# One engine order for another in a gated mix of sliding-window attention and a token-mixing MLP

## The chip, the core and the metric

The kernel runs on one core of a Trainium2 chip. Its time is the device time of one execution in microseconds (us), and the figure that is compared is the median of several executions.

## What is computed

For 2048 tokens of 512 features, an attention `a` (32 heads of 16 features, causal window of 256 tokens) and an MLP `b` that mixes tokens are added with a gate per token:

```python
g = sigmoid((x * gate_w).sum(-1, keepdims=True))          # x: 1 x 2048 x 512
qkv = x @ wqkv                                            # wqkv: 512 x 1536, 32 heads of 16
scores = q @ k.T * 16 ** -0.5, kept where 0 <= i - j < 256
a = (softmax(scores) @ v) @ wo
h = layernorm(x)
u = gelu(einsum("bsd,sf->bdf", h, w1) + b1)               # f = 1376
b = transpose(einsum("bdf,fs->bds", u, w2) + b2)
out = g * a + (1 - g) * b
```

All inputs and the output are bf16.

## The kernel before

The work is cut into some 1100 small tasks, and the order in which each engine takes its tasks is written out by hand as lists of names, one for each engine (`PLAN`): PE is TensorE, ACT is ScalarE, DVE is VectorE, POOL is GpSimd, and SP is the queue that issues all loads and stores. A name may carry the numbers of the buffers that the task takes. `arrange` walks through these lists with a price for each task and emits the instructions engine by engine in that order; the prices decide only how the lists interleave in the program, not what stands in a list. `BLOCK`, `AHEAD`, `FETCH` and `BUSY` are its prices for fetching PE's instructions in blocks of 256; `LATENCY` is its price from an engine's end to the next engine's start.

The tasks, by name (j is one of 17 query stretches of 128 tokens, shifted by 64, the first and the last being halves; t a tile of 128 tokens; i a quarter of 512 tokens):

- `warm`, `warmb`: products of a zeroed tile (`zeros`, a memset on DVE), before the data are there. `xta0.*` transposes the first 512 tokens on PE, `xtc0.*` copies the result to `XT0`; the other quarters are loaded transposed by DMA (`xt1` to `xt3`).
- `x*`, `wqk*`, `wv`, `gw`, `w1_gi`, `w2_g`, `wo`, `bias`: loads. `wqk` holds the weights of q and k in four pieces, `wv` those of v, `gw` the gate's weights copied to all partitions.
- `q`, `k`, `v`, `u`, `y`: chains of full matrix products (`chain`, line 670), cut into steps of two products, each chain in one PSUM bank: `k3_0.2` is the step from product 2 of the third k group of quarter 0. `qc`, `kc`, `vc`, `ub`, `f` evict the bank on ACT or DVE. A step can run with the array tiled in four column groups, which takes four times the instructions; the set `THEN` says after which tasks this is done.
- `s{j}.v*`, `s{j}.C`, `s15.A`, `s15.B`: scores into a pair of PSUM banks, on 32 rows of the array; `e*` takes the exponential on ACT, `m*` the mask (on DVE as a product with a mask tile, or on POOL as an affine select), `pv{j}.*` the product with V. Then `n1` to `n4` and `nz` on DVE transpose, divide by the row sums and transpose back into `xo`.
- `bs`, `ba`, `pow`, `h`: the layer norm. All sixteen `h` are needed before the first `u` chain.
- `y{t}` sums the MLP's second product (11 weight chunks, the last of 96 rows) and the attention's output projection (4 chunks) in one chain of 15 products; `f{t}` applies the gate and bias in one eviction, `o{t}` stores. For the last tile, the chain is cut by columns: `y15l` and `y15r`, 256 columns each.
- The gate's logits: for quarter 0 on PE (`gate0`, 16 products of one column with the transposed `XT0`, line 802, then `gatem0`), for the other quarters on DVE (`gl4` to `gl15`, line 822, a product with `gw` summed over the row). `NGP` is the number of quarters that PE does. `gatee` is the exponential, `ez` spreads it for the attention's division, `gates` forms the two columns for `f`.

PE changes between four modes: full products (d), column-tiled products and `pv` (p), scores (s), corner scores (c); a half `pv` step is a fifth (h).

Of the kernel before, what the change touches and what calls it, by code (L numbers as in the profile page):

```python
# [9 lines left out]
ACT = mybir.ActivationFunctionType  # L10
# [68 lines left out]
SWITCH = 0.095  # L79

BLOCK, AHEAD, FETCH, BUSY = 256, 80, 3.6, 3.0
LATENCY = {"PE": 0.22, "ACT": 0.15, "DVE": 0.12, "POOL": 0.15, "SP": 2.0}


def arrange(tasks):
# [18 lines left out]
    mode, then = "d", "d"  # L104
    count, come, loads = AHEAD, {}, 0.0
    order = []
    while len(order) < len(tasks):
# [19 lines left out]
        t.cost = t.engines[e]  # L127
        ins = t.ins
        if e == "PE":
            new = then if t.flex else t.mode  # L130
            if new != mode:
                t.cost += SWITCH
            if t.flex and new == "p":
                t.tiled = True
                ins *= 4
            if t.mode != "d":
                then = "p" if t.name in THEN else "d"
            mode = new
        if e == "SP" and t.lat is not None and t.engines[e] > 1.0:
            loads = max(loads, start + t.cost + t.lat)  # L140
        if ins:
            block = count // BLOCK
            while (block + 1) * BLOCK <= count + ins:
                block += 1
                at = start + t.cost * (block * BLOCK - count) / ins
                wait = max(0.0, come.get(block, 0.0) - at)
                t.cost += wait
                come[block + 1] = at + wait + FETCH + (BUSY if at + wait < loads else 0.0)
            count += ins
# [41 lines left out]
        warm:3 xta0.0.0:7 xta0.0.1:6 warmb xta0.1.1:4 xta0.1.0:5 q1_0.0:2 k3_0.0:3 k1_0.0:6 q3_0.0:1 k0_0.0:7  # L191
        q3_0.1 q0_0.0:0 k3_0.1 q1_0.1 q1_0.2 k1_0.1 k3_0.2 k0_0.1 q0_0.1 q2_0.0:5 q1_0.3 q0_0.2 q1_0.4 q0_0.3
        k3_0.3 q3_0.2 q0_0.4 k3_0.4 q3_0.3 k2_0.0:4 q2_0.1 k0_0.2 k1_0.2 k1_0.3 k0_0.3 k1_0.4 q2_0.2 q3_0.4 q2_0.3
        k0_0.4 k2_0.1 k2_0.2 k2_0.3 k2_0.4 q2_0.4 s0.v0:62 q3_1.0:0 q3_1.2 k3_1.0:1 k3_1.2 q0_1.0:7 s0.C:42 v1.0:6
        q0_1.2 s-1.C:02 v1.2 v2.0:5 v2.2 s1.v3:02 biast:4 v0.0:7 v0.2 v3.0:5 v3.2 q1_1.0:4 s1.v0:62 v5.0:1 q1_1.2
        gate0:5 v5.2 v14.0:0 s0.v1:62 v13.0:5 k2_1.0:1 v14.2 pv-1.0:6 v10.0:4 k2_1.2 v13.2 s1.v2:26 k2_2.0:0 v10.2
        v15.0:1 v12.0:5 v12.2 v15.2 k2_2.2 pv0.0:2 pv0.1 s1.v1:64 pv0.2 v4.0:1 v4.2 k3_2.0:0 k3_2.2 s2.v1:26 v7.0:5
        v7.2 k0_2.0:4 s1.C:60 k0_2.2 v6.0:3 v6.2 s2.v3:06 k0_1.0:2 k0_1.2 k1_1.0:5 k1_1.2 pv1.0:6 pv1.1 pv1.2
        s2.v0:02 v11.0:4 v11.2 v8.0:5 v8.2 pv1.3 pv1.4 s2.v2:20 q2_1.0:5 v9.0:4 q2_1.2 s2.C:26 v9.2 k1_2.0:1 k1_2.2
        u3.0:0 u3.2 s3.v1:64 u3.4 u3.6 u3.8 s3.C:26 u3.10 u3.12 u3.14 u2.0:1 s3.v2:24 pv2.0:6 pv2.1 u7.0:0 pv2.2  # L200
        pv2.3 u7.2 u2.2 s3.v0:42 u2.4 u7.4 u7.6 s3.v3:46 u7.8 u7.10 u7.12 s4.v0:62 u2.6 u2.8 u2.10 u2.12 u2.14
        s4.v1:24 pv3.0:6 pv3.1 pv3.2 pv3.3 u7.14 u10.0:1 u10.2 s5.v2:42 u10.4 u10.6 u10.8 s4.v3:62 u10.10 q0_2.0:0
        q0_2.2 s4.v2:64 u10.12 u10.14 q3_2.0:2 u0.0:3 q3_2.2 s4.C:06 u0.2 u0.4 u0.6 s6.v0:40 u0.8 u0.10 u0.12
        u6.0:2 u0.14 s5.v0:06 pv4.0:4 pv4.1 pv4.2 pv4.3 u6.2 u6.4 q2_2.0:3 s5.v1:06 u6.6 q2_2.2 u6.8 s5.C:64 u6.10
        u6.12 u5.0:3 s6.C:60 u6.14 u5.2 u5.4 s6.v2:46 u5.6 k3_3.0:2 k3_3.2 q1_2.0:1 q1_2.2 u5.8 s5.v3:46 u5.10
        u1.0:2 u1.2 s6.v1:06 u1.4 pv5.0:4 u5.12 pv5.1 pv5.2 pv5.3 s6.v3:06 u1.6 u5.14 u1.8 s7.v0:64 u1.10 pv6.0:0
        pv6.1 pv6.2 u1.12 pv6.3 s7.v1:64 u1.14 u4.0:3 u4.2 s7.v3:06 u4.4 k1_3.0:2 k1_3.2 s7.C:04 u4.6 u4.8 q0_3.0:2
        s7.v2:60 q0_3.2 u4.10 u4.12 u4.14 s8.v3:46 u9.0:2 u9.2 u9.4 s8.C:04 u8.0:3 u8.2 u8.4 u8.6 s8.v1:46 u8.8
        u9.6 u9.8 s8.v0:04 u8.10 u9.10 u9.12 u8.12 u8.14 s8.v2:06 pv7.0:4 u9.14 pv7.1 pv7.2 pv7.3 s10.v0:02
        k0_3.0:7 k0_3.2 q1_3.0:4 q1_3.2 q3_3.0:6 k2_3.0:5 k2_3.2 q3_3.2 pv8.0:0 pv8.1 pv8.2 pv8.3 y4.0:3 q2_3.0:6  # L210
        q2_3.2 y0.0:7 y0.2 y0.4 y8.0:2 y0.6 y4.2 y0.8 s9.v1:40 y4.4 y8.2 y0.10 y8.4 y0.11 y0.13 s9.v3:40 y4.6 y4.8
        y4.10 y4.11 s9.v2:60 y4.13 y8.6 y8.8 s9.C:04 y7.0:3 y8.10 y7.2 y8.11 s9.v0:60 y7.4 y8.13 y7.6 s10.C:46 y7.8
        y2.0:2 y2.2 s10.v3:06 y2.4 y7.10 y2.6 y7.11 s11.v3:46 y2.8 y7.13 pv9.0:0 pv9.1 pv9.2 pv9.3 s10.v2:64 y2.10
        y2.11 y9.0:3 y9.2 s10.v1:04 y2.13 y9.4 y9.6 s11.C:60 y9.8 y1.0:2 y1.2 s11.v2:40 y1.4 y1.6 y9.10 y1.8
        s11.v1:06 y9.11 y9.13 y1.10 y1.11 s13.v3:04 y1.13 pv10.0:6 pv10.1 pv10.2 pv10.3 s12.v2:02 y5.0:5 y10.0:4
        y10.2 s12.v0:26 y5.2 y10.4 y5.4 y10.6 s11.v0:06 y5.6 y5.8 y5.10 y5.11 s12.v1:02 y10.8 y10.10 y10.11 y5.13
        s12.v3:62 y10.13 pv11.0:0 pv11.1 pv11.2 y3.0:5 pv11.3 s13.v0:26 y3.2 y11.0:4 y11.2 s12.C:60 y3.4 y11.4
        y11.6 s13.C:62 y11.8 y11.10 y11.11 y3.6 s13.v1:20 y11.13 pv12.0:6 y3.8 pv12.1 pv12.2 pv12.3 s14.v3:20 y3.10
        y3.11 y6.0:4 y3.13 s13.v2:26 y6.2 y6.4 y12.0:5 s14.v2:06 y12.2 y12.4 y6.6 s14.v0:02 y6.8 y6.10 pv13.0:6
        pv13.1 pv13.2 y6.11 pv13.3 s14.v1:02 y12.6 y12.8 y6.13 s14.C:26 y12.10 y12.11 y12.13 y13.0:0 y14.0:1 y14.2  # L220
        y13.2 s15.A:62 pv14.0:4 pv14.1 y14.4 pv14.2 pv14.3 y13.4 s15.C:26 y14.6 y13.6 y13.8 s15.B:42 y15l.0:7 y14.8
        y15l.2 y15r.0:6 y15l.4 y15l.6 y13.10 pv15.0:4 y14.10 pv15.1 pv15.2 y15r.2 y15l.8 y15l.10 y15r.4 y13.11
        y14.11 y14.13 y13.13 y15r.6 y15r.8 y15l.11 y15l.13 y15r.10 y15r.11 y15r.13
    """,
    ACT="""
        xtc0.0.1 xtc0.1.0 xtc0.1.1 kc3_0 kc1_0 kc0_0 kc2_0 e0.v0.0:4 e0.v0.1:5 kc3_1 e0.C.1:8 e0.C.0:a e-1.C.1:7
        e-1.C.0:b vc1 vc2 e1.v3.1:2 e1.v3.0:3 vc3 e1.v0.0:6 e1.v0.1:9 vc5 gatee0 e0.v1.0:d e0.v1.1:c vc14 kc2_1
        vc13 e1.v2.1:b e1.v2.0:7 vc12 vc15 kc2_2 e1.v1.0:5 e1.v1.1:a vc4 e2.v1.1:4 e2.v1.0:8 e1.C.1:d e1.C.0:c vc7
        vc6 e2.v3.1:1 e2.v3.0:0 kc1_1 e2.v0.1:a e2.v0.0:9 vc8 vc11 e2.v2.0:b e2.v2.1:5 e2.C.1:e vc9 e2.C.0:f
        e3.v1.0:c e3.v1.1:d e3.C.0:7 e3.C.1:6 ub3 e3.v2.0:a e3.v2.1:4 e3.v0.0:b e3.v0.1:5 e3.v3.1:f e3.v3.0:e  # L230
        e4.v0.1:1 e4.v0.0:0 e4.v1.0:b e4.v1.1:4 ub7 e5.v2.1:f e5.v2.0:e e4.v3.0:a e4.v3.1:d e4.v2.0:5 ub10
        e4.v2.1:c e4.C.0:2 e4.C.1:3 e6.v0.1:9 e6.v0.0:8 gatee1 e5.v0.1:0 e5.v0.0:1 e5.v1.1:c e5.v1.0:d e5.C.0:4
        e5.C.1:5 e6.C.0:7 e6.C.1:6 e6.v2.1:a e6.v2.0:b kc3_3 e5.v3.1:g e5.v3.0:h e6.v1.0:2 e6.v1.1:3 gatee2
        e6.v3.1:g e6.v3.0:h e7.v0.0:f e7.v0.1:e ub5 e7.v1.0:g e7.v1.1:d e7.v3.0:h e7.v3.1:c e7.C.0:9 e7.C.1:8
        e7.v2.0:a e7.v2.1:b e8.v3.0:6 e8.v3.1:7 e8.C.1:3 e8.C.0:4 e8.v1.0:2 e8.v1.1:5 e8.v0.0:1 e8.v0.1:0 gatee3
        e8.v2.0:f e8.v2.1:e e10.v0.0:g e10.v0.1:h gelu e9.v1.1:b e9.v1.0:8 e9.v3.1:9 e9.v3.0:2 e9.v2.1:4 e9.v2.0:3
        e9.C.0:5 e9.C.1:i e9.v0.0:a e9.v0.1:j e10.C.1:6 e10.C.0:f e10.v3.1:0 e10.v3.0:c e11.v3.0:1 e11.v3.1:d
        e10.v2.1:7 e10.v2.0:e e10.v1.0:5 e10.v1.1:4 e11.C.1:3 e11.C.0:j e11.v2.1:b e11.v2.0:a e11.v1.0:i e11.v1.1:2
        e13.v3.0:9 e13.v3.1:8 e12.v2.1:c e12.v2.0:0 e12.v0.1:f e12.v0.0:g e11.v0.0:5 e11.v0.1:e e12.v1.1:4
        e12.v1.0:7 e12.v3.0:h e12.v3.1:e e13.v0.1:d e13.v0.0:6 e12.C.0:1 e12.C.1:j e13.C.1:3 e13.C.0:i e13.v1.0:5  # L240
        e13.v1.1:2 e14.v3.0:j e14.v3.1:b e13.v2.1:c e13.v2.0:f e14.v2.0:e e14.v2.1:a e14.v0.1:7 e14.v0.0:d
        e14.v1.1:h e14.v1.0:i e14.C.0:f e14.C.1:g f12:0 e15.A.1:c e15.A.0:h e15.C.0:j e15.C.1:5 e15.B.0:9 e15.B.1:f
        f14:1 f15l:3
    """,
    DVE="""
        const zeros bs3:1 xtc0.0.0 bs2:0 ba3 parity bs1:1 ba2 ba1 bs0:0 ba0 qc1_0 bs4:1 qc0_0 ba4 qc3_0 qc2_0 qc3_1
        bs8:1 bs9:0 qc0_1 ba8 ba9 bs11:1 biasc vc0 bs5:0 ba11 ba5 bs10:1 bs7:0 ba10 ba7 gatem0 bs14:1 qc1_1 bs6:0
# [1127 lines left out]
```

## Time and profile before

| | |
|---|---|
| median of the runs | 200.57 us |
| the runs | 200.57, 200.81, 199.84 us |
| the profiled execution | 199.82 us, of it a span of 198.1 us |
| granted TensorE clock | 1.00 |
| DMA | 22.02 MB, 36.9% of 16 engines' span on the loads' and stores' queue |
| store of a full tile, 128 KB | 2.4 us from issue to landing |
| last eviction's start | 195.04 us |

The profile page gives each engine's busy time as a share of the span, and the span in 40 slices in which a digit is the busy share in tenths. A line of the waits reads: who waited, for whom, us in total, times, the longest one. A group's line reads: source line, engine, operation, output and input tiles with shape and type, count, then busy us and mean ns of one, then idle us before it and who ended that. Matmuls are pipelined and their ends are modelled, so on PE the distance from start to start says what one costs.

### The profile page before, as it was taken

To read this page: it belongs to the slowest core of one execution; us is meant where nothing else is said; L and a number is where in the kernel's file an instruction comes from. 1 tells how busy PE (TensorE), PEld (TensorE's weight loads), DVE (VectorE), ACT (ScalarE), POOL (GpSimd) and SP (SyncE) were. 2 spreads that over 40 slices of the span, in tenths; PEclk is the share of its full clock that TensorE was granted. 3 is DMA by queue.
4 is the path that set the end of the run, shared out by engine and by line. 5 is a ranking of instruction groups with operands and counts; after the bars stand their busy time and mean duration, and the time that the engine had idled before them with its cause. 6 is when DMAs were issued, how large, how long until landed. Compare 5 with 4: busy or idle time off the path is not lost. (4 is left out here: it accounts for less than half of the span.)

```text
span 198.1 us, 9100 instructions
## 1 busy us (share of the span) xinstructions
PE 193.0 (97%) x4058; PEld 93.3 (47%) x4058; DVE 156.5 (79%) x318; ACT 169.0 (85%) x198; POOL 80.0 (40%) x118
## 2 busy tenths in 40 slices
PE   7999999999999999999999999999999999999993
PEld 3643444353635445446543554344445354554572
DVE  1799888879998988986589799636867868869683
ACT  2369999999988996998999899899899989898632
POOL 6394897525344440214223200045069335452310
PEclk9999999999999999999999999999999999999999
DMA  5999798970060000001399770000211220200002
GB/s 156 294 284 232 131 319 278 346 187 0 8 174 18 18 0 3 3 5 32 98 364 367 280 210 3 26 26 30 68 37 58 60 68 22 62 30 30 30 3 83
DMA packets 23189, 22.02 MB, mean 111 GB/s; under 512 B 7566, under 2 KB 21262, under 8 KB 23150
## 3 DMA queue, kind: packets, MB, share of 16 engines
q1 hardware_dynamic: 23150, 21.44, 36.9%
q8 instruction: 32, 0.52, 1.1%
q14 instruction: 7, 0.06, 0.1%
HBM read 15.61 MB, written 2.10 MB: 89 GB/s over the span
## 5 line engine op out<-in xcount | busy, mean ns | idle before, releaser
L894 ACT ACTIVATE et<-ps 128x1024 bf16<-128x1024 f32 (+1 forms) x94 | 89.3, 1015 | 6.1 <-PE ps L942 2.4
L536 POOL TENSOR_SCALAR_AFFINE_SELECT et<-et 128x512 bf16<-128x512 bf16 (+2 forms) x63 | 46.7, 751 | 56.0 <-ACT et L894 40.9
L894 ACT ACTIVATE XT<-ps 128x1024 bf16<-128x1024 f32 (+1 forms) x60 | 58.1, 1011 | 7.3 <-PE ps L942 4.3
L670 PEld LDWEIGHTS <-wb 128*32 128x32 bf16 (+4 forms) x645 | 32.0, 97 | 34.5 <-issue 6.5
L670 PE MATMUL pb<-ug,wb 128*32 128x512 bf16 (+4 forms) x385 | 45.5, 366 | 0.0
L670 PE MATMUL pb<-h,wb 128*128 128x512 bf16 (+2 forms) x260 | 44.5, 381 | 0.0
L536 POOL TENSOR_SCALAR_AFFINE_SELECT XT<-XT 128x512 bf16<-128x512 bf16 (+1 forms) x28 | 20.0, 720 | 46.3 <-ACT XT L894 27.4
L670 PE MATMUL pb<-XT,wqkv 128*128 128x512 bf16 (+2 forms) x190 | 32.4, 372 | 0.4 <-DMA wqkv<-in_A_wqkv_dram 0.3
L1178 DVE STREAM_TRANSPOSE et<-ps 128x1024 f32<-128x1024 f32 (+1 forms) x17 | 20.1, 1183 | 11.9 <-PE ps L1087 11.1
L1087 PEld LDWEIGHTS <-VA 128*32 128x32 bf16 (+1 forms) x1056 | 20.1, 97 | 6.6 <-issue 1.5
L942 PE MATMUL ps<-QZ,KT 32*128 32x256 bf16 (+1 forms) x496 | 23.1, 265 | 0.0
L754 DVE TENSOR_TENSOR QZ<-pb,par 128x1024 bf16<-128x1024 f32 x16 | 19.5, 1221 | 3.2 <-PE pb L670 3.2
L670 PEld LDWEIGHTS <-wqkv 128*128 128x128 bf16 (+1 forms) x190 | 12.7, 98 | 14.6 <-DMA wqkv<-in_A_wqkv_dram 0.5
L670 PE MATMUL pb<-wo,xo 128*32 128x512 bf16 (+2 forms) x152 | 18.1, 375 | 0.0
L1087 PE MATMUL ps<-et,VA 128*32 128x128 bf16 (+2 forms) x624 | 17.9, 218 | 0.0
L942 PEld LDWEIGHTS <-KT 32*128 32x128 bf16 x496 | 7.4, 92 | 20.6 <-ACT et L894 10.7
L670 PE MATMUL pb<-wqkv,XT 128*128 128x512 bf16 (+1 forms) x70 | 16.5, 381 | 0.0
L974 DVE TENSOR_TENSOR et<-et,mask 128x512 bf16<-128x512 bf16 x26 | 13.3, 510 | 2.5 <-ACT et L894 2.4
L441 DVE TENSOR_SCALAR ot<-pb,c,c 128x512 bf16<-128x512 f32 (+1 forms) x11 | 8.6, 785 | 7.4 <-PE pb L670 7.3
L1087 PE MATMUL ps<-XT,VA 128*32 128x128 bf16 (+2 forms) x432 | 13.9, 215 | 0.0
L1087 PEld LDWEIGHTS <-VZ 128*32 128x32 bf16 x832 | 13.2, 98 | 0.7
L770 DVE BATCH_NORM_STATS2 stats<-xo 128x6 f32<-128x512 bf16 x16 | 10.7, 682 | 3.1 <-DMA xo<-in_A_x_dram 3.1
(76 smaller groups left out, 199.4 us busy)
## 6 DMA issues: line engine op xcount, KB each, us to landing
wb<-in_B_w_dram SPq DMA_DIRECT2D x8, 512.0 KB, 8.2
wb<-in_B_w_dram SPq DMA_DIRECT2D x2, 2048.0 KB, 9.2
VZ<-VA SPq DMA_DIRECT2D x26, 70.0 KB, 3.0
xo<-in_A_x_dram SPq DMA_DIRECT2D x3, 512.0 KB, 5.5
out_dram<-ot SPq DMA_DIRECT2D x12, 128.0 KB, 2.4
wb<-in_B_w_dram SPq DMA_DIRECT2D x4, 352.0 KB, 5.8
wqkv<-in_A_wqkv_dram SPq DMA_DIRECT2D x4, 256.0 KB, 5.0
wb<-in_B_w_dram SPq DMA_DIRECT2D x1, 1024.0 KB, 5.3
```

The source lines that it names most:

```text
L441: return nc.vector.tensor_scalar(out=out_, in0=in_, scalar1=scale, scalar2=bias, op0=ALU.mult, op1=ALU.add)
L536: return nc.gpsimd.affine_select(out=out_, in_=in_, pattern=[[0, n] for n in pattern] + [[step, HB]], compare_op=op, fill=0.0, base=base_, ...
L670: made.append(nc.tensor.matmul(buf(b)[c:z_, c0:c0 + w_], lhsT=lhsT[:, c:z_], rhs=rhs, start=(j == 0), stop=(j == n - 1), skip_group_check= ...
L754: lambda k=k, b=b: nc.vector.tensor_tensor(out=QZ[:, k, :, (i % NQ) * SB:(i % NQ + 1) * SB], in0=buf(b)[:, None, :].to_broadcast([P, 2, SB ...
L770: f"bs{t_}", {"DVE": 0.67}, lambda b=b, t_=t_: nc.vector.bn_stats(buf(b)[:], xo[:, t_, :]),
L894: lambda e=e, b=b, shape=shape: nc.scalar.activation(out=shape(buf(e)), in_=shape(buf(b)), func=ACT.Exp, scale=SCALE),
L942: made.append(nc.tensor.matmul(to[:, :, done:done + m], lhsT=keys(j if x == "A" else j - 1, k)[rows], rhs=q[rows], start=True, stop=True, ...
L974: made.append(nc.vector.tensor_tensor(out=v, in0=v, in1=m.to_broadcast(list(v.shape)), op=ALU.mult))
L1087: return lambda: nc.tensor.matmul(to(), lhsT=v() if callable(v) else v, rhs=buf(e)[rows, col:col + n], start=first, stop=last, tile_positi ...
L1178: lambda: nc.vector.transpose(out=view(buf(tr).bitcast(FP32)), in_=view(buf(o))), [last], takes=[tr], uses=[o],
```

## The change

- `NGP` goes from 1 to 0: the logits of the first 512 tokens come from four `gl` tasks on DVE instead of `gate0` on PE, and the load `gw` moves ahead of `wv` in SP's list.
- The last tile's output is cut into 256, 128 and 128 columns (`y15l`, `y15m`, `y15r`) with an eviction and a store for each.
- The tile that the warming products read is 128 columns instead of 512, repeated by a stride of zero; its memset stands ahead of `const` in DVE's list.
- All five lists and `THEN` are new. 76 tasks change engine: net, 25 masks go from POOL to DVE (POOL 83 to 58, DVE 70 to 95); three `kc` go from DVE to ACT and three `vc` the other way; one `ub` goes from DVE to ACT. PE has 3984 matmuls instead of 4058.
- The planner's prices change: a price for each pair of PE modes, DVE tasks 0.06 cheaper, a model of block fetch with `AHEAD` and `INSIDE`.

```diff
-SWITCH = 0.095
-
-BLOCK, AHEAD, FETCH, BUSY = 256, 80, 3.6, 3.0
-LATENCY = {"PE": 0.22, "ACT": 0.15, "DVE": 0.12, "POOL": 0.15, "SP": 2.0}
+TURN = {
+    "d": dict(d=0, s=0.100, p=0.100, c=0.098, h=0.100),
...
+BLOCK, AHEAD, INSIDE, FETCH, BUSY = 256, 77, 194, 4.0, 2.4
+LATENCY = {"PE": 0.21, "ACT": 0.15, "DVE": 0.11, "POOL": 0.12, "SP": 2.3}
+
+def cost_of(t, e):
+    c, n = t.engines[e], t.name
+    if e == "PE":
+        return c - 0.02 if t.mode == "s" else c * 0.738 if t.mode == "c" else c
+    if e == "DVE":
+        return max(0.1, c - 0.06)
...
 PLAN = dict(
     PE="""
-        warm:3 xta0.0.0:7 xta0.0.1:6 warmb xta0.1.1:4 xta0.1.0:5 q1_0.0:2 k3_0.0:3 k1_0.0:6 q3_0.0:1 k0_0.0:7
...
-        k0_0.4 k2_0.1 k2_0.2 k2_0.3 k2_0.4 q2_0.4 s0.v0:62 q3_1.0:0 q3_1.2 k3_1.0:1 k3_1.2 q0_1.0:7 s0.C:42 v1.0:6
...
+        warm:3 xta0.0.1:6 xta0.0.0:4 warmb xta0.1.0:7 xta0.1.1:6 k3_0.0:4 k3_0.1 q0_0.0:0 q0_0.1 q3_0.0:3
...
+        q0_0.4 k2_0.2 k3_0.4 k0_0.4 v1.0:3 v1.2 q2_0.3 q2_0.4 s0.v0:06 v0.0:4 k2_0.3 k2_0.4 v0.2 v5.0:5
...
+        y15l.2 y15r.2 y15r.4 y14.11 y14.13 y15l.4 y15r.6 y15l.6 y15l.8 y15l.10 y15l.11 y15l.13 y15m.0:4
+        y15r.8 y15r.10 y15m.2 y15r.11 y15r.13 y15m.4 y15m.6 y15m.8 y15m.10 y15m.11 y15m.13
...
     DVE="""
-        const zeros bs3:1 xtc0.0.0 bs2:0 ba3 parity bs1:1 ba2 ba1 bs0:0 ba0 qc1_0 bs4:1 qc0_0 ba4 qc3_0 qc2_0 qc3_1
...
+        zeros const parity bs1:1 ba1 bs2:0 ba2 bs0:1 bs3:0 xtc0.1.1 qc3_0 ba3 qc1_0 ba0 qc0_0 bs7:0 h1 qc2_0
...
     SP="""
-        x0.0 x0.2 wqk0 wqk1 wqk2 wqk3 x1.4 xt1 wv x2.8 bias xt3 x3.12 xt2 vs0 w1_02 w1_03 vs1 w1_22 vs2 gw w1_12
...
+        x0.0 x0.2 wqk0 wqk1 wqk2 wqk3 gw wv x1.4 xt1 xt3 x2.8 bias vs0 xt2 x3.12 vs1 w1_00 w1_01 vs2 w1_10
+        w1_11 w1_03 w1_13 w1_22 w1_02 w1_23 w1_12 w1_20 vz4:1 vz2:2 vz3:0 w1_21 vz5:2 vz6:0 vz7:1 w2_0 w2_1
...
-    NGP = 1
+    NGP = 0
...
-    zeros = ug[:, 0, :]
+    zeros = ug[:, 0, 0:P]
...
-            nc.tensor.matmul(buf(wu)[:, 0:w], lhsT=zeros[:, 0:P], rhs=zeros[:, 0:w], start=True, stop=True)
+            nc.tensor.matmul(
+                buf(wu)[:, 0:w].rearrange("p (a b) -> p a b", b=P), lhsT=zeros,
+                rhs=zeros[:, None, :].to_broadcast([P, w // P, P]), start=True, stop=True,
+            )
...
-        parts = [("", 0, D)] if t_ < NT - 1 else [("l", 0, D // 2), ("r", D // 2, D)]
+        parts = [("", 0, D)] if t_ < NT - 1 else [("l", 0, D // 2), ("m", D // 2, 3 * D // 4), ("r", 3 * D // 4, D)]
```

## The prediction

> **What bounds the kernel now.** I read the busy shares and the slices of the page first, then what TensorE (PE) waited for, then PE's starts one after another, and last the busy table of the stretch in which most of the attention overlaps the projections.
>
> ```profile
> PE 193.0 (97%) x4058; PEld 93.3 (47%) x4058; DVE 156.5 (79%) x318; ACT 169.0 (85%) x198; POOL 80.0 (40%) x118
> PE   7999999999999999999999999999999999999993
> q8 instruction: 32, 0.52, 1.1%
> ```
>
> PE has work in every slice but the first and the last. The waits of PE itself, as the trace names them, are all:
>
> ```profile
> PE pb L591 <- DVE ug L518: 1.4, 1, 1.4
> PE pb L670 <- DMA wqkv<-in_A_wqkv_dram: 0.3, 1, 0.3
> PE pb L670 <- ACT XT L894: 0.2, 1, 0.2
> ```
>
> A busy PE may still be stretched, so I read the starts in its timeline (start, length, engine, line, tiles, count):
>
> ```profile
> 46.75 1.03 PE L670 MATMUL pb<-h,wb 128*128 128x512 bf16 x4
> 47.71 0.40 PE L942 MATMUL ps<-QZ,KT 32*128 32x256 bf16 x8
> 48.04 1.47 PE L670 MATMUL pb<-h,wb 128*128 128x512 bf16 x6
> ...
> 112.98 0.40 PE L942 MATMUL ps<-QZ,KT 32*128 32x256 bf16 x8
> 113.56 1.77 PE L670 MATMUL pb<-XT,wqkv 128*128 128x512 bf16 x7 [0.18 <-ACT XT L894]
> ```
>
> Six 512-column products alone start 0.2155 us apart. From 46.75 to 47.71 there are 0.96 us for four, so the change of the array's mode from full products to scores costs 0.96 - 0.862 = 0.10 us. Eight score products take 0.33 us with the change back; at 112.98 the same eight take 0.58, a true wait of 0.25. Done for all PE tasks (each against the usual step of its kind and its successor), the true waits after the first projection at 6.57 sum to only about 1.0 us: 0.25 there, 0.13 at 142.9, two of 0.08 among the first two projections, 0.08 at 114.0, 0.07 at 144.8, and a tail of 0.03 to 0.05. The rest of the way from 6.57 to 195.0 is work in PE's order plus 169 changes of mode. So a new order can win at most the work it removes, its mode changes and this 1.0 us; it can lose without limit.
>
> ```profile
> 25.00:54.00 29.00, 29.00 (x586) 13.01 (x588) 25.91 (x63) 28.35 (x38) 16.24 (x23) 1.00 0.63 192
> ```
>
> Columns: window, length, busy us of PE, PEld, DVE, ACT, POOL, clock, DMA share, GB/s. Here PE is full, ScalarE (ACT) 98% and VectorE (DVE) 89%: the engines behind PE have little room.
>
> **The change, part by part, on PE.**
> Gate logits: gate0's 16 one-column products run from 23.02 to 23.43, 0.40 us, all on PE's path. They go: -0.40. Four logits more on DVE cost 4 x (0.695 + 0.081) = 3.1 us of DVE, in the stretch 16 to 21; their readers (gatee0, ez0, the first nz) come ten us later, so nothing on PE waits for them.
>
> ```profile
> 23.02 0.54 PE L802 MATMUL pb<-gwc,XT 128*128 128x1 bf16 x16
> 23.43 0.38 PE L670 MATMUL pb<-wqkv,XT 128*128 128x512 bf16 x1
> ```
>
> Order on PE: the new order has 167 changes of mode instead of 169: -0.2. It has 62 column-tiled chain steps instead of 74, so 7976 PE instructions instead of 8116. The 32 packets of the instruction queue are one for every 256 instructions; in the trace of before they took 0.9 to 1.5 us each and no PE wait falls on a block's start. So the fetch price in the planner has nothing to save here: 0, with ends -0.1 and +0.5 (two waits of the largest size seen, 0.25, if the new bursts outrun the fetch).
>
> Last tile: y15's right half of 256 columns becomes two chains of 128, 15 products each; one 96-row step each counts with them. From 190.98 to 195.01 there are 28 products in 4.04 us, eight of 512 columns: (4.04 - 8 x 0.2155) / 20 = 0.116 for one of 256, with the mode's and the last one's drain in it; 0.109 is the usual start to start. No 128-column full product runs warm in this trace. Below, it costs half, 0.054; above, as much as one of 256, 0.109. With 15 more products the added time is 0 to +1.6 us. I take 0.056 (the line through 256 and 512 columns), +0.05 in sum, since gate0 shows a full weight load with a product every 25 ns, so the load is not the limit. The Trainium skill ("TensorE: Matmul & The Clock Gate", section "Back-to-back issue gap") speaks against this: it puts streams of weight load and 128-column product at about 81 ns each; by it the two chains would cost 0.75 us more, an estimate.
>
> After PE's end the last eviction is on the path.
>
> ```profile
> 193.62 0.81 DVE L441 TENSOR_SCALAR ot<-pb,c,c 128x512 bf16<-128x512 f32 x1 [0.25 <-PE pb L670]
> 195.04 0.55 DVE L441 TENSOR_SCALAR ot<-pb,c,c 128x256 bf16<-128x256 f32 x1 [0.61 <-PE pb L670]
> ```
>
> 256 columns less save 0.26, so 128 less save 0.13 (0.42). f15l, f15r and f15m now all stand on DVE; f15r's 0.42 fits in the 0.6 us of products between its chain's end and y15m's. One more store is issued, 0.33 us on the queue, while the last chain runs. The last store falls from 64 KB to 32 KB, from rows of 512 bytes to 256: no row shows such a store to DRAM. The stores of 64 KB landed in 1.5 us, the usual 128 KB in 2.2; bounds -0.1 and +0.7, and I take 0.
>
> Start: zeros moves ahead of const and fills a quarter, so the warming products begin up to 0.3 us sooner. The path does not: the first projection waits for wqkv's landing at 6.57, and the queue to there is unchanged. What can be won are the 0.16 us by which the first two 256-column products exceed 0.109. I take -0.1 (ends 0 and -0.16).
>
> Queue: gw (128 KB) and wv (512 KB) now stand ahead of x1.4 and xt1. Before, x1.4 landed at 10.1 and XT1 at 12.1, 1.9 us apart; 640 KB more put wv near 10.6, x1.4 near 12.4 and XT1 near 14.4. In the new order the sum of PE's rows puts the first reader of wv (v1.0) at 12.6 and of XT1 (v5.0) at 15.7: covered by 1.3 us; gone, each us late is a us on PE. w1_02, now the eighth of the w1 pieces, has until u3.0 at 45.8; before, the pieces there landed by 41.7.
>
> **DVE, ACT, POOL.** 25 masks go from POOL (153 in all, 83 there before, 58 after) to DVE.
>
> ```profile
> L536 POOL TENSOR_SCALAR_AFFINE_SELECT et<-et 128x512 bf16<-128x512 bf16 x45 | 30.7, 694 | 31.3 <-ACT et L894 19.5 <-DVE junk L822 4.4 <-DVE h L786 2.2
> L974 DVE TENSOR_TENSOR et<-et,mask 128x512 bf16<-128x512 bf16 x26 | 13.3, 510 | 2.5 <-ACT et L894 2.4
> ```
>
> On DVE one is 0.33 us start to start in a full queue, 0.51 by the mean row, which holds stays behind POOL. So DVE gains 8 to 13 us and the logits' 3.1: about 170 of 198. Copies only change places (three K copies to ACT, three V copies to DVE). The tight place is from n1-1 (end of pv-1) to n12 (end of pv2): DVE's starts sum to 23.6 us before and, with 19 tasks in and 10 out, to 27.6 after; PE's sum there is 28.0. It fits by 0.4, and the next thing late would be the last h tasks and with them u3.0, which needs all 16. I cost it at nothing, with an end of +2.3 below.
>
> **Sum.** -0.40 - 0.2 + 0.05 - 0.13 - 0.1 = -0.8, with true waits on PE staying at 1.0. The profiled run is span 198.1 + 1.7 around it = 199.82, so 199.0 on its own scale; it was the quickest of those shown, 0.75 below the median, and I put the change to the median: 200.57 - 0.8 = 199.8.
>
> **The rivals.**
> Waits shrink too. The search may remove most of the 1.0 us as well: 0.8 of it gives 199.0. For it: the new prices of DVE tasks in the diff (0.06 less) lie near the starts in the trace. Against: 0.25 is the largest single wait there is to find.
>
> DVE's queue becomes the bound, the case on the other side. Place: n1-1 to n12, and again on each of the next three visits up to u's end, where DVE's share of PE's time is 0.84 to 0.93. Price: five masks there at 0.51 instead of 0.33 are 0.9 us, 0.5 more than the room; u3.0 and the scores behind it wait, and four such places make 2.2 us: 200.57 - 0.8 + 2.2 = 202.0. It decides once true waits on PE pass 1.8 us (no gain) or 2.8 (slower by 0.5%). For it: DVE near 98% with ACT at 98%. Against: POOL is emptier by 17 us, so masks on DVE should stay behind POOL less.
>
> The change doesn't do what it says. Small pieces at the end cost what they save: 30 products at 0.082, the middle of the two bounds, instead of 0.056 are 0.8: 200.6.
>
> **How the numbers follow.** 0.5%, 1.0 us, is about what a measurement of this kernel can tell from no change. The forecast, waits 0.6 to 1.5, spans 199.3 to 200.3: chance 0.50, of it 0.19 beyond 0.5%. Waits shrink: 0.16, all faster. DVE bound: 0.24, 0.20 slower, 0.04 within. End pieces: 0.10, within but for 0.02. Faster 0.35, same 0.43, slower 0.22. The range goes from 198.8 to 202.0; it leaves out a DVE lag of more than four places and a perfect order.
>
> **What would show it.** Right: no one-column products on PE, 167 mode changes, first projection at 6.5 to 6.6, last eviction near 0.42 us, y15m's products 0.056 apart, PE's end near 194.3. DVE as bound: u3.0 later than 46.4, PE idle or stretched scores between 46 and 90. End pieces: steps of 0.08 or more in y15m, more than 2.5 us from the last eviction's start to the span's end. It is wrong altogether if PE's true waits sum to over 1.8 us, or if XT1 lands after 15.7.

## The result, and the profile after

| | before | after |
|---|---|---|
| median, us | 200.15 (20 runs, 199.50 to 200.81) | 200.48 (20 runs, 199.99 to 203.38) |
| ratio to before, 95% interval | | 1.0022 [1.0006, 1.0038] |

The change makes the kernel slower by 0.2%. That is less than the 0.5% bound, and it lies inside the range, but the forecast was 199.8, on the other side. The first profile of the changed kernel fell on its one slow execution (203.38 us, which the ratio leaves out); I show what only it has, and read the rest from a later profile of the same kernel, of 200.32 us, called a_third. Line numbers of the changed kernel are 38 higher in most places (670 is 708, 942 is 980, 1087 is 1125, 536 is 571). Its page (a_third):

```profile
PE 192.6 (97%) x3984; PEld 92.9 (47%) x3984; DVE 161.6 (81%) x351; ACT 169.2 (85%) x199; POOL 57.2 (29%) x91
...
PE   6999999999999999999999979999999999999994
...
PEclk9999999999999999999999999999999999999999
...
q8 instruction: 31, 0.51, 1.1%
...
L1012 DVE TENSOR_TENSOR et<-et,mask 128x512 bf16<-128x512 bf16 x44 | 18.4, 432 | 3.8 <-ACT et L932 3.6
```

PE has 74 matmuls fewer and is 0.4 us less busy. One slice, the 24th, has fallen from 9 to 7. DVE has 5 us more work, not the 8 to 13 for the masks and 3 for the logits that I allowed: a mask of this form takes 432 ns in the mean instead of 510, so 44 of them take 18.4 us where 26 took 13.3. What PE waited for (a_third):

```profile
PE ps L1125 <- issue: 1.1, 1, 1.1
PE pb L626 <- DVE ug L553: 1.0, 1, 1.0
PE pb L646 <- DMA xo<-in_A_x_dram: 0.5, 1, 0.5
PE ps L1125 <- POOL et L571: 0.3, 1, 0.3
PE pb L708 <- ACT XT L640: 0.3, 1, 0.3
```

Two lines of this list from behind the first microseconds have no counterpart before, the first and the fourth. "issue" means that PE waited for nothing that the profile shows: no engine, no data. In the first profile it is longer:

```profile
PE ps L1125 <- issue: 2.2, 1, 2.2
...
PE ps L1125 <- POOL et L571: 0.3, 1, 0.3
```

Where it is, in the first profile's timeline of PE:

```profile
117.57 0.23 PE L1125 MATMUL ps<-et,VA 128*32 128x128 bf16 x2 [2.19 <-issue]
...
118.59 4.45 PE L708 MATMUL pb<-XT,wqkv 128*128 128x512 bf16 x12
```

and in that of a_third:

```profile
116.66 0.23 PE L1125 MATMUL ps<-et,VA 128*32 128x128 bf16 x2 [1.09 <-issue]
...
117.69 2.76 PE L708 MATMUL pb<-XT,wqkv 128*128 128x512 bf16 x12
```

The stop is in the middle of `pv7.3`. After the longer one, 12 products take 4.45 us that take 2.76 in a_third; the granted clock of the window from 113 to 124 is 0.84 there (0.50 from 118.6 to 122.0), and 1.00 in a_third. So a stop of 2.2 us cost 1.7 us more behind itself, and one of 1.1 us nothing.

The balance from before's profile (199.82 us, span 198.1) to a_third (span 198.6), with each PE task held against the usual step of its kind as in the prediction. The first row is counted with these steps, and the last but one is what is left over, so that the rows add up to the spans; it is more than the 1.0 us of true waits that the prediction counted before:

| | predicted | measured |
|---|---|---|
| work in PE's order: gate0, changes of mode, last tile | -0.55 | -0.55 |
| start: first projection 6.57 to 6.12, and 0.41 more wait at its second product | -0.1 | -0.05 |
| last matmul to last store's issue, 0.88 to 0.69 | -0.13 | -0.19 |
| last store's issue to the span's end, 2.49 to 2.34 | 0 | -0.15 |
| the stop in pv7.3 | 0 | +1.28 |
| pv0.0, behind GpSimd's masks | 0 | +0.45 |
| all other stretching of PE, 1.53 to 1.24 | 0 | -0.29 |
| sum | -0.8 | +0.5 |

Five terms came as foreseen or a little better. The loss is in the two that were put at nothing, above all in the stop.

### The profile page after: what moved, and what is told of

It reads as the page before. It is cut to its first block, busy times and chain, and to the rows that moved or that the text cites. A ratio compares the mean times of both kernels' runs of the same rounds, so it can differ in the third digit from the quotient of the medians.

```text
span 201.7 us, 8941 instructions
## 1 busy us (share of the span) xinstructions
PE 194.5 (96%) x3984; PEld 93.3 (46%) x3984; DVE 161.9 (80%) x351; ACT 169.2 (84%) x199; POOL 57.1 (28%) x91
## 4 chain that ended last, share of the span: by engine, by line
PE 89%; DMA 3%; ACT 2%; issue 2%; POOL 2%; DVE 0%; DVEq 0%; SPq 0%; POOLq 0%
PE pb L708 65%; PE ps L1125 10%; PE ps L980 9%; PE ps L1080 3%; DMA out_dram<-junk 2%; POOL et L571 2%; ACT et L932 1%; DMA xo<-in_A_x_dram 1%; PE pb L646 1%; ACT ot L473 0%; PE ps L1036 0%; PE pb L626 0%; ACT VA L640 0%; DVE ot L476 0%; SPq L1343 0%
## 5 line engine op out<-in xcount | busy, mean ns | idle before, releaser
L932 ACT ACTIVATE et<-ps 128x1024 bf16<-128x1024 f32 (+1 forms) x102 | 96.6, 1009 | 12.1 <-PE ps L980 7.7
L571 POOL TENSOR_SCALAR_AFFINE_SELECT et<-et 128x512 bf16<-128x512 bf16 (+2 forms) x46 | 31.9, 703 | 80.1 <-ACT et L932 56.0
L932 ACT ACTIVATE XT<-ps 128x1024 bf16<-128x1024 f32 (+1 forms) x52 | 51.5, 1028 | 3.7 <-PE ps L980 2.3
L708 PEld LDWEIGHTS <-wb 128*32 128x32 bf16 (+3 forms) x613 | 32.7, 97 | 36.4 <-issue 6.1
L708 PE MATMUL pb<-h,wb 128*32 128x512 bf16 (+2 forms) x292 | 44.3, 381 | 0.0
L571 POOL TENSOR_SCALAR_AFFINE_SELECT XT<-XT 128x512 bf16<-128x512 bf16 (+1 forms) x18 | 11.8, 658 | 48.1 <-ACT XT L932 28.3
L708 PE MATMUL pb<-wo,xo 128*32 128x512 bf16 (+3 forms) x138 | 17.9, 368 | 0.0
L708 PE MATMUL pb<-wqkv,XT 128*128 128x512 bf16 x64 | 17.2, 380 | 0.0
L1216 DVE STREAM_TRANSPOSE et<-ps 128x1024 f32<-128x1024 f32 (+1 forms) x12 | 14.4, 1197 | 2.7 <-POOL et L571 1.3
L476 DVE TENSOR_SCALAR ot<-pb,c,c 128x512 bf16<-128x512 f32 (+2 forms) x11 | 8.1, 747 | 7.8 <-PE pb L708 7.8
```

Of the source, the lines that this page charges most:

```text
L476: return nc.vector.tensor_scalar(out=out_, in0=in_, scalar1=scale, scalar2=bias, op0=ALU.mult, op1=ALU.add)
L571: return nc.gpsimd.affine_select(out=out_, in_=in_, pattern=[[0, n] for n in pattern] + [[step, HB]], compare_op=op, fill=0.0, base=base_, ...
L708: made.append(nc.tensor.matmul(buf(b)[c:z_, c0:c0 + w_], lhsT=lhsT[:, c:z_], rhs=rhs, start=(j == 0), stop=(j == n - 1), skip_group_check= ...
L932: lambda e=e, b=b, shape=shape: nc.scalar.activation(out=shape(buf(e)), in_=shape(buf(b)), func=ACT.Exp, scale=SCALE),
L1216: lambda: nc.vector.transpose(out=view(buf(tr).bitcast(FP32)), in_=view(buf(o))), [last], takes=[tr], uses=[o],
```

## Experiments

**What is the stop?** Theory: PE waits for its own instructions. They come in packets, one for each 256 instructions. Between the place where the next packet is asked for (in the planner's model 77 instructions ahead of a block) and the place where PE needs it, the new order has some 260 instructions (4001 to 4260) that run in 3.3 us; in the order before, the same numbers take 5.5 us. Rival, from the prediction: VectorE's queue is the bound. The first run is the changed kernel again.

> The changed kernel itself, once more, for a second profile of it. In the first profile PE stood 2.4 us inside pv7.3 at 115.2 with no data to wait for, then ran at half clock for four steps (1.7 us more), and stood 0.44 us in pv0.0 for POOL's masks. Fetch theory (PE runs out of fetched instructions in the dense stretch pv7.3/pv8, block 17 of 256): the stop comes back at the same instruction (4260th, in pv7.3), 0.5 to 2.5 us long, and the time is 200.0 to 201.0. Rival 1 (the queues of DVE and ACT are the bound, and the stop was an accident of one execution): no stop in pv7.3, and the loss against before is spread over waits of scores and pv for ACT, DVE and POOL. Both: 0.4 us in pv0.0.

Measured: 200.71 us, ratio 1.0032 [1.0020, 1.0044]; PE stopped again in pv7.3, for 0.96 us there and 0.26 in pv8.3. Of its list of waits:

```profile
PE pb L708 <- issue: 4.3, 27, 0.2
...
PE ps L1125 <- issue: 0.8, 1, 0.8
PE pb L708 <- ACT XT L640: 0.4, 1, 0.4
```

The first line is no stop: this trace has 3951 records of matmuls for 3984 weight loads, and where single records are missing the list shows 27 gaps of at most 0.2 us. The traces of a_plus14, a_plus88 and a_plus14_pool lack 33 records each as well and have the same line. The stop in pv7.3 belongs to the kernel, and its length varies.

Then 14 instructions more at the start, before any real work: seven products of 32 columns behind the warming ones.

```diff
-    add("warm", {"PE": 2.2}, lambda: warming(5, 512), [kz], takes=[wu], ins=10)
+    add("warm", {"PE": 2.2}, lambda: warming(5, 512) + tiny(7), [kz], takes=[wu], ins=10)
```

> Seven products of 32 columns more at the end of the warming, so that every later PE instruction stands 14 places further on in the blocks of 256; nothing else changes, and PE idles there anyway. In the changed kernel the two tiled steps of u10, whose chunk has 96 rows, take 12 instructions each and not the 16 that the planner counts, so from there on PE stands 8 places earlier in its blocks than planned. Fetch theory: the stop in pv7.3 goes or falls below 0.8 us (from asking to needing the block there are 4.2 us instead of 3.1), and the time falls by 0.5 to 1.0 us against the changed kernel, to about 199.6. Rival 1 (DVE, ACT and POOL): the same time as the changed kernel within 0.2 us, since no work of theirs changes.

Measured: 201.19 us, ratio 1.0057 [1.0035, 1.0080]. A miss for the theory: the time didn't fall, and whether it rose against a_again the two intervals can't tell; the time alone would fit the rival too. What it shows all the same is where PE stops:

```profile
PE ps L986 <- issue: 0.9, 1, 0.9
PE ps L1131 <- issue: 0.8, 1, 0.8
```

Line 1131 is `pv` and line 986 the scores. The old stop has moved from pv7.3 into the task ahead of it, pv8.2, and is at the same instruction number. A new one has come in s2.v0. The distance from request to need at the old place had grown from 3.3 to 4.3 us, by the theory enough to shorten the stop to under 0.8 us; but the packet landed at 116.04 in this profile and at 114.99 in that of a_again, 1.05 us later. With 88 instructions more (three long warming products and 46 short ones), many blocks end in dense stretches:

```diff
+    add("warm", {"PE": 2.2}, lambda: warming(3, 512) + tiny(46), [kz], takes=[wu], ins=10)
```

> As before this one, but with 46 products of 32 columns in place of two of the five warming products: every later PE instruction stands 88 places further on. The work is the same. Fetch theory: now the dense stretches of several visits (about 73, 92, 114, 147 and 166 us) fall between a block's asking and its need, with 1.4 to 2.0 us where a fetch takes about 4; PE stops several times by 2 to 4 us, and the time rises by 6 to 17 us to 206 to 217. Rival 1: no more than 0.5 us.

Measured: 207.69 us, ratio 1.0386 [1.0344, 1.0428], for the same work with the same data in the same order. From its list of waits:

```profile
PE ps L1131 <- issue: 3.7, 2, 2.2
PE ps L986 <- issue: 2.3, 2, 1.7
```

The engines behind PE have the same work as in the changed kernel; what has moved is the place of the blocks' edges. The four stops sum to 6.0 us, and 3.4 us at a granted clock of 0.50 follow the last one (124.7 to 128.1). I counted the instruction (twice the weight loads) at which PE resumed, for every gap of over 0.8 us between its weight loads after 20 us, in all profiles taken up to the end. The trace also has each packet of instructions as a transfer, 31 or 32 on the queue "instruction"; the last column holds the resumption against the landing of the packet that came last:

| kernel | resumed at instruction | that number modulo 256 | us after the packet landed |
|---|---|---|---|
| changed kernel, its repeats, a_pool_ot | 4264 in all four | 168 | 1.39, 1.42, 1.52, 1.45 |
| a_plus14, a_plus14_pool | 948 and 4264 in both | 180, 168 | 1.48, 1.40; 1.29, 1.31 |
| a_plus88 | 2476, 3496, 4264, 4520 (and 4562) | 172, 168, 168, 168 (and 210) | 1.32, 1.39, 1.44, 1.35 |
| b_tail | 6816 | 160 | 1.47 |
| a_spread, a_spread_pool_ot, best_again, before | none | | |

Thirteen of fourteen lie 160 to 180 instructions behind a multiple of 256. The fourteenth, in brackets, is no stop: the list of waits has none there, and it lies at the end of the 3.4 us at half clock. A late operand or an engine behind would not know this number, nor when a packet of instructions lands; PE resumed 1.3 to 1.5 us after it all thirteen times.

**The wait at pv0.0.** Three masks of stretch 1 stand ahead of m0.v1.0 on GpSimd. In this run they go behind it, on top of the 14 instructions.

```diff
-        ident masks ones blanks pow0 m0.v0.0 m-1.C.0 m-1.C.1 m0.v0.1 m1.v0.0 m1.v3.1 m1.v0.1 m0.C.1 m0.C.0
-        m0.v1.1 m0.v1.0 m1.v2.0 ...
+        ident masks ones blanks pow0 m0.v0.0 m-1.C.0 m-1.C.1 m0.v0.1 m0.C.1 m0.C.0
+        m0.v1.1 m0.v1.0 m1.v0.0 m1.v3.1 m1.v0.1 m1.v2.0 ...
```

> With the seven products, and three masks of visit 1 moved behind the last masks of visit 0 in POOL's list. Both theories: the 0.44 us in pv0.0 shrinks to 0.1 or less. If PE is the bound from there on, the time falls by another 0.3 us to about 199.3; if DVE and ACT are the bound between 30 and 55, PE waits there instead and the time stays.

Measured: 200.96 us, ratio 1.0040 [1.0020, 1.0060]. The wait of 0.45 at pv0.0 is gone, and both stops for instructions have stayed. The medians differ by 0.23, less than the two intervals can tell apart; the profile's first projection was late by a load, at 7.24.

**Taking the stop away without moving the block's edges.** The number of instructions up to 4001 and from some 500 later on is kept; only the dense stretch is spread.

```diff
-        u9.12 u9.14 q1_3.0:4 pv7.2 s10.v0:06 q1_3.2 k2_3.0:5 k2_3.2 pv8.0:6 pv8.1 pv8.2 pv7.3 pv8.3 q3_3.0:5
-        q3_3.2 q2_3.0:4 k0_3.0:0 k0_3.2 q2_3.2 s9.v1:26 y0.0:1 y4.0:0 y0.2 y0.4 y0.6 y4.2 y4.4 y4.6 y4.8
+        u9.12 u9.14 q1_3.0:4 pv7.2 s10.v0:06 q1_3.2 k2_3.0:5 k2_3.2 pv7.3 k0_3.0:0 k0_3.2 q3_3.0:5
+        q3_3.2 q2_3.0:4 q2_3.2 pv8.0:6 pv8.1 pv8.2 pv8.3 y0.0:1 y4.0:0 y0.2 y0.4 s9.v1:26 y0.6 y4.2 y4.4 y4.6 y4.8
...
-        m8.v2.1 qc1_3 kc2_3 n18:g n17:8 kc0_3 n27 qc2_3 qc3_3 nz7:1 n28
+        m8.v2.1 qc1_3 kc2_3 n17:8 n27 kc0_3 qc3_3 n18:g qc2_3 nz7:1 n28
...
 THEN: s10.v0 out, s9.v2 in
```

> The changed kernel with one stretch of PE's order spread out: pv7.3 directly behind k2_3, then k0_3, q3_3 and q2_3, and only then pv8.0 to pv8.3 (DVE's n17, n27 and n18 follow). The three k and q steps behind s10.v0 go untiled (36 instructions fewer) and the three y steps behind s9.v2 tiled (36 more), so every instruction behind them keeps its number. Between instruction 4001 (where the block that holds 4260 is asked for) and 4260 there are now some 5.5 us of work where there were 2.9. Theory (PE waits for its own instructions at 4260): the stops in pv7.3 (0.96) and pv8.3 (0.26) of the repeat go, no other takes their place, and the two changes of mode and a short wait for a bank cost back 0.3 to 0.5: 200.7 - 1.2 + 0.4 = 199.9, range 199.6 to 200.3. Rival (the stop belongs to the time of the 2 MB load or to a clock dip, whatever PE executes): about 1 us stays near 115 to 117 us, 200.7 to 201.3. Rival (DVE is what bounds this stretch): DVE's later n18 delays s9.v1 and more, 201 or above.

Measured: 200.21 us, ratio 1.0012 [0.9986, 1.0038]. No stop is left: the packet for instruction 4264 landed at 116.85, no sooner after instruction 4001 (3.0 us) than in a_again (3.0), but PE came to that instruction only at 120.30, 3.5 us behind the landing. pv7.3 has the short wait that was allowed for (0.21), and a y step 0.23. The profiled execution was the slowest of its runs (202.37): its first 14 products of 256 columns started 0.21 us apart instead of 0.11, a loss at the start that is not the stretch's. The intervals of this run and of the changed kernel overlap; what is shown is that the stop is gone. Then the same with GpSimd's order mended, and with a fifth output buffer (`gwr`, read for the last time long before) for the eviction f15l, which in the repeat a_again had waited for an earlier store:

```diff
-f15l:0 f15r:1 f15m:3
+f15l:4 f15r:1 f15m:3
...
+    otr.tiles.append(gwr)
```

> As the spread kernel, and the two other losses of the repeat removed: m1.v0.0, m1.v3.1 and m1.v0.1 go behind m0.v1.0 on GpSimd (pv0.0's wait of 0.37), and the eviction f15l gets a fifth output buffer (the gate-weight row, dead by then), so it waits for no store. Theory: the spread kernel's time less 0.3 to 0.4 for pv0.0 and less 0.3 for the tail (last matmul to last store issue 0.7 where the repeat had 1.02): 199.2, range 198.8 to 199.7, the first of these kernels that is faster than the one before (200.1). Rival (what is removed at pv0.0 is waited for elsewhere, and the tail is set by the queue of SP and not by the buffer): same as the spread kernel, 199.6 to 200.3.

Measured: 199.50 us, ratio 0.9969 [0.9957, 0.9980]: inside the range, and faster than before. That run's end shows the third piece alone behind PE, in VectorE's timeline and in the queue's:

```profile
195.36 0.41 DVE L477 TENSOR_SCALAR junk<-pb,c,c 128x128 bf16<-128x128 f32 x1 [0.21 <-PE pb L709]
```

```profile
195.18 0.33 SPq L1344 DMA_DIRECT2D out_dram<-ot  x1
195.79 0.33 SPq L1344 DMA_DIRECT2D out_dram<-junk  x1
```

In a_again the tail was a queue of evictions behind a store, in place of that (VectorE):

```profile
194.96 0.86 DVE L476 TENSOR_SCALAR ot<-pb,c,c 128x256 bf16<-128x256 f32 x2 [1.24 <-DMA out_dram<-ot]
195.74 0.41 DVE L476 TENSOR_SCALAR junk<-pb,c,c 128x128 bf16<-128x128 f32 x1
```

There the last matmul to the last store's issue took 1.02 us and nothing was won; in a_third the store was early enough (0.69).

**The last tile alone, in the order before.**

```diff
-y15r.10 y15r.11 y15r.13
+y15r.10 y15r.11 y15r.13 y15m.0:2 y15m.2 y15m.4 y15m.6 y15m.8 y15m.10 y15m.11 y15m.13
```

> The kernel before with one part of the change alone: the last tile in pieces of 256, 128 and 128 columns, in the kernel before's own order (the third piece's products last, its eviction on VectorE, with an output buffer of its own: the gate-weight row). No instruction ahead of the last tile moves. Theory of the prediction: +0.05 for the products (14 of 128 columns at 0.056 for 7 of 256 at 0.11), -0.13 for the eviction (0.55 to 0.42), nothing for the store: last matmul to last store issue falls from 0.88 to about 0.7, time 200.0 against 200.1, within 0.2 of the kernel before. Rival (the pieces cost more than they save: products at 0.081 give +0.35, or a third store in SP's queue at 0.4): 200.3 to 200.6.

Measured: 200.15 us, ratio 1.0009 [0.9994, 1.0023]: no difference that can be told. (The 14 and 7 products of the text above should be 30 and 15, which give its +0.05.) The tail itself did what was said, 0.73 from the last matmul to the last store's issue instead of 0.88. But this profiled execution had a stop of its own, far ahead of the last tile, in instructions that are those of before, number for number:

```profile
171.93 0.39 PE L946 MATMUL ps<-QZ,KT 32*128 32x256 bf16 x6
173.24 0.28 PE L946 MATMUL ps<-QZ,KT 32*128 32x256 bf16 x2 [0.92 <-issue]
```

In before's profile the 252 instructions ahead of this place took 3.0 us as well, and PE didn't stop. What differs is the packet: it landed at 170.50 there, 1.6 us ahead of the need at 172.09, and at 171.77 here, where PE resumed 1.47 us later. So the order before runs close to this edge too; that its own executions pass it at times is likely, but its one profile doesn't show it.

**Which repair gives how much.** The last three runs were made side by side on one chip: the changed kernel, the same with GpSimd's order and the fifth buffer mended, and the one with all three.

> The changed kernel again, in one call with the others, for the comparison: 200.4 to 200.8, PE's stop at instruction 4260 in the profile, 0.9 to 2.4 long.

> The changed kernel with GpSimd's order and the fifth output buffer mended, and PE's dense stretch left as it is. Theory: pv0.0's wait goes (0.4) and the tail is shorter (0.3), but PE still stops at instruction 4260 for 0.9 to 1.3: 200.6 - 0.7 = 199.9, range 199.7 to 200.4, some 0.5 above the spread kernel with both mended (199.5). Rival (those two losses were all of it, and the spreading only moved a stop that cost nothing in most executions): the same time as the spread kernel with both mended, within 0.15.

> The spread kernel with GpSimd's order and the fifth buffer mended, again, beside the other two: 199.3 to 199.7, 0.9 to 1.2 below the changed kernel; no stop of PE for its own instructions.

| kernel | median us | ratio to before |
|---|---|---|
| changed kernel, a_third | 200.41 | 1.0026 [1.0010, 1.0042] |
| GpSimd's order and buffer, a_pool_ot | 199.78 | 0.9988 [0.9969, 1.0007] |
| these and the spread stretch, best_again | 199.44 | 0.9959 [0.9943, 0.9975] |

The two small repairs are worth 0.63, the spread 0.34 more, somewhat less than the 0.5 expected. The intervals of the last two overlap; that the stop is gone is seen in the profiles. a_pool_ot still has it, and the last kernel has products of full width in the same place:

```profile
116.20 0.23 PE L1128 MATMUL ps<-et,VA 128*32 128x128 bf16 x2 [0.82 <-issue]
```

```profile
114.69 2.76 PE L709 MATMUL pb<-XT,wqkv 128*128 128x512 bf16 x12
117.39 0.41 PE L1126 MATMUL ps<-et,VA 128*32 128x128 bf16 x16
```

## Why the prediction was wrong

**The step that failed** is "the fetch price in the planner has nothing to save here: 0, with ends -0.1 and +0.5". It measured +1.28 in a_third, about 1.2 in a_again, and 2.4 with 1.7 of slow clock behind it in the first profile. I read from before's trace that no wait of PE falls on a block, and took this for a property of PE. It was one of that order, and a close one: at four blocks (93.8, 97.2, 172.1 and 180.3 us) PE came to the block about 1.2 to 1.6 us after its packet had landed, hardly more than the 1.3 to 1.5 us after which it resumed from the stops. What had to be counted is in the two lists: the instructions from request to need, and the time that the new order gives them. With pv7.2 to pv8.3 nearly in a row these are 3.3 us at 112 us, while w2 is being loaded; with 62 tiled steps instead of 74, all later edges lie elsewhere too (the trace has 7968 weight loads and matmuls; the prediction's 7976 counts two steps with 8 too many). The end of +0.5 came from the largest data wait of the trace, and was the row of another thing.

**True waits on PE stay at 1.0.** They did not: +0.45 at pv0.0. I weighed POOL by its load (17 us less) and not by its order, in which three masks of the next stretch precede the one that PE needs first.

**The work on PE** was right, -0.55 when it is counted with the usual steps: no one-column product is left, and there are 167 changes of mode. No wait of PE in a_third names the loads of `wv` and `xt1`, so the queue cost nothing, as predicted. The end pieces are settled as well. Seven products of 128 columns of y15m (a_third, start and count):

```profile
195.00 0.56 PE L708 MATMUL pb<-ug,wb 128*128 128x128 bf16 x7
195.40 0.39 PE L708 MATMUL pb<-wo,xo 128*128 128x128 bf16 x4
```

0.40 / 7 = 0.057 each, against 0.056 predicted. The Trainium skill ("TensorE: Matmul & The Clock Gate", section "Back-to-back issue gap") has about 81 ns for this case; the measurement decides. The rival that rested on dear end pieces falls; that its 200.6 lies near the result is chance.

**The last eviction** is 0.41 (0.42 predicted), and the store of 32 KB was no slower to the span's end than that of 64 KB.

**VectorE as the bound** fell. Its share of the window from 25 to 54 rose from 25.91 to 27.07 us of 29, as I feared, yet u's first product starts earlier than before, at 46.59, not later:

```profile
25.00:54.00 29.00, 28.73 (x590) 12.88 (x592) 27.07 (x70) 27.90 (x39) 15.58 (x25) 1.00 0.72 214
```

```profile
46.59 1.03 PE L708 MATMUL pb<-h,wb 128*128 128x512 bf16 x4
47.55 0.40 PE L980 MATMUL ps<-QZ,KT 32*128 32x256 bf16 x8
```

No wait of PE in a_third names DVE but the one for the zeroed tile. "Wrong altogether if true waits sum to over 1.8" is what came true, by a wait of which the rivals held none.

**What stays open.** The packets' transfers themselves took 1.0 to 1.2 us at this place, and PE went on 1.3 to 1.5 us after them; the rest of the delay lies ahead of them. From instruction 4001, where the planner's model has the request, to the packet's start it was 2.0 to 3.2 us in the changed kernel. In a_third the four packets that started between 100 and 118 us, while w2 and other data were loaded, came 2.1 to 3.3 us after that point of their blocks, and the others after 50 us 0.2 to 1.7 us. So the loads are the likely cause of the late packet, but the place of the request is the model's, and no run moved the loads by themselves.

## What to carry to other kernels

When an order is changed on an engine with thousands of instructions, count them: for each block, the time from request to need is a resource like a buffer, and the densest stretch decides, not the mean. Before reading a slower time as a data wait, look for "issue" in the engine's waits, and whether it returns at the same instruction number when something is put ahead of it. And weigh a queue by what stands ahead of the one task that is waited for, not by how full it is.

## What the runs showed of the hardware

Instructions put at the very start, which cost nothing themselves, moved the stops of PE: with 14 more it stopped at one more place (201.19 us against 200.71, a difference that the intervals don't settle), and with 88 more the median was 207.69. In all thirteen stops PE resumed 1.3 to 1.5 us after its packet of 256 instructions had landed. After the two longest, of 2.2 us (the first profile and a_plus88), the granted clock was 0.50 for 3.4 us; in the first profile that cost 1.7 us. After stops of 0.8 to 1.1 us (a_third, a_pool_ot) the next products ran at the full one. The time of the first projection varied from 6.04 to 7.24 us between executions of nearly the same kernels; in five of the eleven profiles other than before's PE waited 0.6 to 1.3 us there for the landing of wqkv.
